# Moving batch 1's attention stretches within block 0, and summing four pairs' squares on ScalarE

## The chip, the core and the metric

The kernel runs on one core of a Trainium2 chip. The metric is the device time of one execution in microseconds (us): the median of three runs. One execution was also profiled, and all rows below come from that one.

Engines are named as in the profile: PE is TensorE (PEld its weight loads), DVE is VectorE, ACT is ScalarE, POOL is GpSimd, and SP is the engine whose queue issues most DMAs. Each engine takes its instructions strictly in the order in which they stand in its queue.

## The reference, cut to what matters

```python
# batch 8, heads 8, seq 576, head_dim 64, d_model 512, d_ff 2048, rank 32
kv  = einsum('bhsd,bhse->bhde', k, v)
out = einsum('bhsd,bhde->bhse', q, kv)
rms = sqrt(mean(out * out, axis=-1) + 1e-06)
x   = (out / rms * g_norm)            # then heads joined: (batch, 576, 512)
h   = x^T @ U @ V                     # mixes over the sequence, rank 32
u   = x + h^T
y   = u + maximum(u @ w_ch1, 0) @ w_ch2
```

The weights arrive as 64-bit floats and are decoded to 32-bit floats on the chip, then split in a high and a low part, so that each product takes three matmuls (high by high, high by low, low by high).

## The kernel before, in words

The 8 batches of 576 rows make 4608 rows, cut into blocks of 512. Blocks 0 to 2 are multiplied directly; the six later blocks in three stages by a scheme with seven products (names P1 to P7), whose weights are made during blocks 0 to 2 and stored to DRAM.

In blocks 0 to 2 a loop runs over the 16 chunks `f` of d_ff. One turn of it is 12 matmuls of the first layer of chunk `f` (lines L484 to L486 before), then relu and its remainder (`hh` on ACT at L496, `hl` on DVE at L501), then 12 matmuls of the second layer of chunk `f - 1` (L508). In block 0 the raw weights of a chunk are decoded during the loop, two to three chunks ahead: copies on ACT (`L167`, `L168`, and the high part `ws` at `L258`), and on DVE the steps L153 to L164 and the low part at `L262`. For chunks 10 and up SP also stores the decoded weights to DRAM (`wf`, L270); the buffer `dec` has two places in turn, so the copy that starts the decoding of chunk 12 waits for the store of chunk 10, and so on. Chunks 0 to 4 are worked off ahead of the loop in an order written out by hand. PE's order is the order of the code; the order on ACT and DVE is set by a list scheduler that works with its own estimate of the times.

Between these matmuls lies the attention of the next batches, pair of heads by pair. Pair (1, 2) is batch 1, heads 4 and 5. A *stretch* (`run(before, now, after)`) puts three things on PE one after another: the rank-32 product `t` of the pair before (L387, L390; it needs that pair's normalised `x`), the kv product of the pair after (L300) and the out product of the pair now (L319). Behind them ACT copies kv and out from PSUM (`kvb` L181, `x` L329), squares `x` into `xt` (L333), DVE sums the squares (L348), ACT takes the root and the half (L349, L350), DVE the reciprocal and one Newton step (L351, L343 to L345) and scales `x` (L363). DVE then turns `x` into the same `xt` (L377), and SP sends it through DRAM into `ut` (L380, L382). `t4_step` makes the factor `t` of the mix from the rank-32 product (ACT L400, L403, L405; DVE L401, L404, L406).

A *mix* (`mix_step`) is two matmuls of a pair's `t` with V (L463), whose results DVE adds to `ut` (L470), and a split of the sum (ACT L422, DVE L423). Stretches and mixes take turns with the two PSUM banks of one pool, so each waits until the one before has been read out.

A slot (j, n) of the tables RUNS and MIXES is the place in block j after quarter n of its chunks: n = 4f + i, where i = 0 is the middle of the first layer of chunk f, 1 its end, 2 the middle of the second-layer matmuls and 3 the end of the turn. From j = 3 on, n counts the units of the stages, of six matmuls each. The first entry of RUNS has no out product. So `t` of (1, 1) stands in the stretch named (1, 2), `t` of (1, 2) in the one named (1, 3), and `t` of (1, 3) in the one named (2, 0).

Of the kernel before, what the change touches and what calls it, by code (L numbers as in the profile page):

```python
# [10 lines left out]
F32 = mybir.dt.float32  # L11
# [4 lines left out]
AF = mybir.ActivationFunctionType  # L16
ALU = mybir.AluOpType
AX = mybir.AxisListType

B, H, S, D = 8, 8, 576, 64  # L20
DM, DF, R = 512, 2048, 32
P = 128
NPAIR = H // 2
NT = 5
# [8 lines left out]
QO = [0, 160, 320, 448]  # L33
ORDER = np.concatenate([np.arange(32) + P * i + 32 * a for a in range(4) for i in range(QL[a] // 32)])
NATIVE = 2
NC = 3
PAIRS = 3
KEEP = 4
FROM_DRAM = 5
COMBOS = [(1, f) for f in (1, 2, 4, 5, 7, 8, 10, 11, 13, 14)] + [(2, f) for f in (4, 5, 7, 8, 10, 11)]  # L40
RUNS = [((1, 0), (0, 20)), ((1, 1), (0, 28)), ((1, 2), (0, 37)), ((1, 3), (0, 45)), ((2, 0), (0, 54)),
# [4 lines left out]
MIXES = {(1, 0): ((0, 26),), (1, 1): ((0, 43),), (1, 2): ((0, 51),), (1, 3): ((0, 60),),  # L46
# [46 lines left out]
def build(ctx: ExitStack, tc: tile.TileContext, kv_in, kvt0_in, kvt_in, q_in, uv_in, g_in, w_in, out):  # L93
    nc = tc.nc
# [7 lines left out]
    sm = ctx.enter_context(tc.tile_pool(name="sm", bufs=2))  # L102
# [96 lines left out]
    def load_kv(b, p):  # L199
# [6 lines left out]
        nc.sync.dma_start(out=kt, in_=kv_in[b, p])  # L206
        if b >= NATIVE:
            tt = ldp.tile([P, 2 * P], F32, name="kvt_sb")
            nc.sync.dma_start(out=tt, in_=kvt_in[b - NATIVE, p])
            loads["t", b, p] = tt  # L210
# [91 lines left out]
    def kv_product(b, p, to):  # L302

        m = loads.pop(("kv", b, p))
        t = loads.pop(("t", b, p))
        by_heads(to, m, t, TAIL * (p % 2) if b < NATIVE else None)

    state = {}
# [16 lines left out]
    def squares(b, p):  # L325
        s = state[b, p]
        x = s["x"]
        for t, lo in zip(s["heads"], (0, D)):
            nc.scalar.activation(out=x[:, :, lo:lo + D], in_=t, func=AF.Copy if s["raw"] else AF.Square)  # L329
        if s["raw"]:  # L330
            xt = s["xt"] = sc.tile([P, 4, NT, 32], F32, name="xt")
            s["x2"] = xt.rearrange("p k i j -> p (k i j)").rearrange("p (i c) -> p i c", c=P)
            nc.scalar.activation(out=s["x2"], in_=x, func=AF.Square)  # L333

    def stats_parts(b, p):

        NS = 2 * NT
        sums, half, r0, ta = [sm.tile([P, NS], F32, name=n) for n in ("sums", "half", "r0", "ta")]
        xv = state[b, p]["x2"].rearrange("p i (h e) -> p i h e", e=D)
        state[b, p]["r"] = half.rearrange("p (i h) -> p i h", h=2)  # L340

        def newton():
            nc.vector.tensor_tensor(out=ta, in0=r0, in1=half, op=ALU.mult)  # L343
            nc.vector.tensor_tensor(out=ta, in0=ta, in1=r0, op=ALU.mult)
            nc.vector.scalar_tensor_tensor(out=half, in0=ta, scalar=1.5, in1=r0, op0=ALU.add, op1=ALU.mult)  # L345

        return dict(
            red=lambda: nc.vector.tensor_reduce(out=sums.rearrange("p (i h) -> p i h", h=2), in_=xv, axis=AX.X, op=ALU.add),  # L348
            ta=lambda: nc.scalar.activation(out=ta, in_=sums, func=AF.Sqrt, scale=1.0 / D, bias=eps[:, 0:1]),  # L349
            hf=lambda: nc.scalar.activation(out=half, in_=sums, func=AF.Identity, scale=-0.5 / D, bias=eps[:, 1:2]),  # L350
            rc=lambda: nc.vector.reciprocal(out=r0, in_=ta),  # L351
            nw=newton)
# [105 lines left out]
    def mix_part(b, p, part):  # L458
# [7 lines left out]
        if b > 2 and not (b in UPPER and part == 1):  # L466
            q = (S * b - BLK * NC) // (2 * BLK)
            at = S * b - BLK * NC - 2 * BLK * q
            to = x32(q)[p][:, at + lo:at + hi]
# [41 lines left out]
    def finish(y, j):  # L511
        uh, ul = ut[j]
        last_block = j == NC - 1
        kept = {}
# [27 lines left out]
    def x32(q):  # L542

        return [t[:, i] for t in x32_tiles(q) for i in range(2)]

    def carry(b, p):

        n = UPPER[b]
        q = (S * b + S - n - BLK * NC) // (2 * BLK)
        if b == 2:  # L550
# [161 lines left out]
    def end_unit(q, n, w):  # L712
# [17 lines left out]
        def leave(c, cols, queue):  # L730
            queue.dma_start(out=out[NC + 2 * q, 2 + c][:, cols], in_=ys[1][:, c, cols])

        if name != "P4":
            for c in range(2):
                products(c, slice(0, BLK), [(kk, w, hs)])
            if kk == KEEP - 1:
# [5 lines left out]
                if name == "P7":  # L742
                    nc.vector.tensor_tensor(out=ys[0], in0=ys[0], in1=spare("P5"), op=ALU.add)
                    for c in range(2):
                        nc.sync.dma_start(out=out[NC + 2 * q + 1, 2 + c], in_=ys[0][:, c])
            return
# [155 lines left out]
    def spread_v(n, eng):  # L902
# [4 lines left out]
        out=uv, in_=uvraw.bitcast(U32).rearrange("p (n t) -> p n t", t=2)[:, :, 1].bitcast(F32), func=AF.Abs)  # L907
# [153 lines left out]
    def run(before, now, after):  # L1061
# [4 lines left out]
        if after:  # L1066
            kv = (two if after[0] < NATIVE and after[1] % 2 else one)[:, BLK - D:]
            kv_product(*after, kv)
# [71 lines left out]
    for j in range(NC):  # L1140
# [3 lines left out]
        for f in range(FIRST if j == 0 else 0, NF):  # L1144
# [5 lines left out]
            h = (ps_h if f % 2 else pools["two"]).tile([P, BLK], F32, name="h")  # L1150
# [111 lines left out]
```

## Time and profile before

| | |
|---|---|
| median of three runs | 837.13 us (836.72 to 837.36) |
| the profiled execution's own time | 837.33 us |
| its span, first to last instruction | 835.6 us |
| PE busy | 820.7 us, 98% of the span, 5492 instructions |
| DVE busy | 585.4 us, 70% |
| ACT busy | 443.4 us, 53% |
| POOL busy | 80.3 us, 10% |
| mean granted TensorE clock | 0.995 |

The times of the runs are a little longer than the span, since they hold what lies ahead of the first instruction and behind the last. Shares of busy time are means over the whole span; the stages differ, so the rows below are cut out of block 0, where all but one of the moved pieces lie.

### The profile page before, as it was taken

The page shows a single profiled execution, that of the slowest core. Times are in us where ns is not written, and L with a number is a line of the kernel's source. Part 1 is how long each engine was busy: PE and PEld are TensorE (multiplying, and loading weights), DVE is VectorE, ACT ScalarE, POOL GpSimd, SP SyncE. Part 2 cuts the span into 40 slices and gives each one's busy share as a digit, 9 for nine tenths or more (in the row PEclk, how much of TensorE's full clock was granted, in tenths as well). Part 3 has the DMA queues.
Part 4 walks back from the last instruction along what each step waited for, and adds up shares of the span by engine and source line. Part 5 has one row for each costly group of instructions (what it writes and reads, how often), then busy time and mean ns, then how long its engine had stood idle before and what let it go on. Part 6 is the DMA issues. An engine that isn't in the chain of part 4 may idle for free.

```text
span 835.6 us, 14368 instructions
## 1 busy us (share of the span) xinstructions
PE 820.7 (98%) x5492; PEld 673.2 (81%) x5492; DVE 585.4 (70%) x1016; ACT 443.4 (53%) x810; POOL 80.3 (10%) x159
## 2 busy tenths in 40 slices
PE   8999799999999999999999999999999999999998
PEld 7777678888888888888888888788888888888887
DVE  5999885888776678666785688568736943582376
ACT  5978752544443445365645664656346724542462
POOL 3002214244330221000000000000000000000000
PEclk9999999999999999999999999999999999999999
DMA  9984767699887779467777768667555685555554
GB/s 346 415 340 144 225 200 226 219 321 277 262 252 266 239 214 316 160 236 262 241 264 236 264 238 282 231 204 242 178 187 196 207 281 197 182 196 195 202 200 153
DMA packets 66357, 198.39 MB, mean 237 GB/s; under 512 B 8176, under 2 KB 27376, under 8 KB 55536
## 3 DMA queue, kind: packets, MB, share of 16 engines
q1 hardware_dynamic: 57184, 167.97, 58.9%
q0 software_dynamic: 8960, 29.37, 10.5%
q8 instruction: 43, 0.70, 0.3%
q14 instruction: 26, 0.21, 0.1%
q10 hardware_dynamic: 144, 0.13, 0.0%
HBM read 146.84 MB, written 50.59 MB: 236 GB/s over the span
## 4 chain that ended last, share of the span: by engine, by line
PE 83%; DVE 6%; DMA 6%; ACT 3%; issue 1%; SPq 0%; ACTq 0%; DVEq 0%
PE yy L671 25%; PE yy L773 23%; PE y L508 13%; PE h L484 5%; PE h L485 5%; PE h L486 4%; DMA w1raw<-w_in 2%; PE ya L723 2%; DMA out<-x 1%; DMA raw<-w_in 1%; PE pp L300 1%; PE pp L319 1%; DVE dec L164 1%; PE h L300 1%; DVE uc L575 1%
## 5 line engine op out<-in xcount | busy, mean ns | idle before, releaser
L671 PE MATMUL yy<-uc,wt 128*128 128x512 f32 x1008 | 234.1, 391 | 0.9 <-ACT t L405 0.9
L671 PEld LDWEIGHTS yy<-uc,wt 128*128 128x128 f32 x1008 | 188.0, 188 | 40.7 <-ACT t L405 1.3
L773 PE MATMUL yy<-dec,wt 128*128 128x512 f32 x468 | 113.8, 391 | 0.3 <-DVE dec L662 0.3
L508 PE MATMUL y<-hh,ws 128*128 128x512 f32 x336 | 113.4, 393 | 0.0
L773 PE MATMUL yy<-hh,wt 128*128 128x512 f32 x312 | 103.3, 390 | 0.0
L773 PEld LDWEIGHTS yy<-dec,wt 128*128 128x128 f32 x468 | 87.2, 188 | 18.9 <-DVE dec L662 0.7
L662 DVE TENSOR_TENSOR hl<-hk,hh 128x512 fp32r<-128x512 f32 x72 | 48.1, 686 | 39.7 <-ACT hh L701 39.5
L662 DVE TENSOR_TENSOR dec<-hk,dec 128x512 fp32r<-128x512 f32 x72 | 48.9, 686 | 37.1 <-ACT dec L701 36.7
L508 PEld LDWEIGHTS y<-hh,ws 128*128 128x128 f32 x336 | 63.1, 188 | 13.8
L773 PEld LDWEIGHTS yy<-hh,wt 128*128 128x128 f32 x312 | 58.6, 188 | 12.4
L484 PE MATMUL h<-ut,ws 128*128 128x512 f32 x168 | 67.5, 402 | 0.0
L485 PE MATMUL h<-ut,ws 128*128 128x512 f32 x168 | 66.6, 396 | 0.0
L486 PE MATMUL h<-ut,ws 128*128 128x512 f32 x168 | 66.4, 395 | 0.0
L508 PE MATMUL y<-hl,ws 128*128 128x512 f32 x168 | 65.8, 391 | 0.0
L773 PE MATMUL yy<-hl,wt 128*128 128x512 f32 x156 | 60.7, 389 | 0.0
L701 ACT CAST dec<-hk 128x512 fp32r<-128x512 f32 x72 | 44.2, 621 | 29.0 <-PE yy L773 14.9
L701 ACT CAST hh<-hk 128x512 fp32r<-128x512 f32 x72 | 44.0, 622 | 27.0 <-PE yy L773 22.8
L659 ACT COPY sp<-yy 128x1024 f32<-128x1024 f32 x35 | 35.5, 1014 | 32.6 <-PE yy L671 25.3
L496 ACT ACTIVATE hh<-h 128x512 fp32r<-128x512 f32 x48 | 28.4, 591 | 36.8 <-PE h L486 36.6
L684 ACT ACTIVATE hk<-hk 128x1024 f32<-128x1024 f32 x24 | 25.5, 1061 | 36.3 <-DVE hk L683 36.3
L659 ACT COPY yy<-yy 128x1024 f32<-128x1024 f32 x17 | 17.0, 998 | 43.4 <-PE yy L671 40.5
L501 DVE SCALAR_TENSOR_TENSOR hl<-h,hh 128x512 fp32r<-128x512 f32 x48 | 32.7, 682 | 9.4 <-ACT hh L496 9.4
(237 smaller groups left out, 1348.0 us busy)
## 6 DMA issues: line engine op xcount, KB each, us to landing
wt<-wd SPq DMA_DIRECT2D x84, 1024.0 KB, 4.9
kv_sb<-kv_in SPq DMA_DIRECT2D x29, 512.0 KB, 5.9
raw<-w_in SPq DMA_DIRECT2D x14, 1023.6 KB, 14.9
wd<-dec POOLq DMA_DIRECT2D x44, 256.0 KB, 5.7
wd<-ws POOLq DMA_DIRECT2D x42, 256.0 KB, 4.0
q_sb<-q_in SPq DMA_DIRECT2D x29, 288.0 KB, 6.3
ut<-xd SPq DMA_DIRECT2D x28, 288.0 KB, 4.1
out<-x SPq DMA_DIRECT2D x23, 256.0 KB, 4.6
```

The source lines that it names most:

```text
L484: nc.tensor.matmul(h, lhsT=w1s[f][0][:, d, :], rhs=uh[d], start=(n == 0), stop=False)
L485: nc.tensor.matmul(h, lhsT=w1s[f][0][:, d, :], rhs=ul[d], start=False, stop=False)
L486: nc.tensor.matmul(h, lhsT=w1s[f][1][:, d, :], rhs=uh[d], start=False, stop=(n == ND - 1))
L496: last["relu"] = nc.scalar.activation(out=last["hh"], in_=h, func=AF.Relu)
L501: last["low"] = nc.vector.scalar_tensor_tensor(out=hl, in0=h, scalar=0.0, in1=last["hh"].bitcast(F32), op0=ALU.max, op1=ALU.subtract)
L508: nc.tensor.matmul(acc, lhsT=w2s[f][w][:, c, :], rhs=h[:, cols], start=(f == 0 and w == 0 and h is hh), stop=(f == NF - 1 and w == 1))
L659: last["unit"] = nc.scalar.copy(out=pair_bank("P6") if name == "P1" else spare(name), in_=acc)
L662: return nc.vector.tensor_tensor(out=out, in0=a, in1=b, op=ALU.subtract)
L671: nc.tensor.matmul(acc[:, i], lhsT=w[:, ws_, e * P:(e + 1) * P], rhs=u[:, e, us], start=name in ("P1", "P5") and e == 0 and k == 0, stop=e ...
L684: last["unit"] = nc.scalar.activation(out=to, in_=to if other else acc, func=AF.Relu)
L701: last["unit"] = nc.scalar.copy(out=hh, in_=src)
L773: nc.tensor.matmul(acc[:, c], lhsT=w[:, ws_, c * P:(c + 1) * P], rhs=h, start=name in ("P1", "P5") and kk == 0 and i == 0, stop=kk == KEEP ...
```

## The change

Three tables and two functions change. In RUNS four stretches of block 0 move to earlier slots: (1, 1) from 28 to 25, (1, 2) from 37 to 33, (1, 3) from 45 to 41 and (2, 0) from 54 to 50; in stage 4 the stretch (7, 2) moves from 18 to 20. In MIXES the mixes of batch 1 move to later slots: 26 to 30, 43 to 45, 51 to 54 and 60 to 61. For the four pairs in SUMMED the one square over 128 x 640 and the sum on DVE are replaced by ten squares over 128 x 64 on ACT, each of which also gives the sum of its 64 results.

```diff
+SUMMED = ((1, 1), (1, 2), (1, 3), (2, 0))
...
-RUNS = [((1, 0), (0, 20)), ((1, 1), (0, 28)), ((1, 2), (0, 37)), ((1, 3), (0, 45)), ((2, 0), (0, 54)),
+RUNS = [((1, 0), (0, 20)), ((1, 1), (0, 25)), ((1, 2), (0, 33)), ((1, 3), (0, 41)), ((2, 0), (0, 50)),
...
-        ((6, 3), (3, 72)), ((7, 0), (3, 84)), ((7, 1), (4, 7)), ((7, 2), (4, 18)), ((7, 3), (4, 29)), (None, (4, 40))]
-MIXES = {(1, 0): ((0, 26),), (1, 1): ((0, 43),), (1, 2): ((0, 51),), (1, 3): ((0, 60),),
+        ((6, 3), (3, 72)), ((7, 0), (3, 84)), ((7, 1), (4, 7)), ((7, 2), (4, 20)), ((7, 3), (4, 29)), (None, (4, 40))]
+MIXES = {(1, 0): ((0, 30),), (1, 1): ((0, 45),), (1, 2): ((0, 54),), (1, 3): ((0, 61),),
...
-            nc.scalar.activation(out=s["x2"], in_=x, func=AF.Square)
+            if (b, p) not in SUMMED:
+                nc.scalar.activation(out=s["x2"], in_=x, func=AF.Square)
+                return
+            sums = s["sums"] = sm.tile([P, 2 * NT], F32, name="sums")
+            for i in range(NT):
+                for h in range(2):
+                    part = slice(h * D, (h + 1) * D)
+                    nc.scalar.activation(out=s["x2"][:, i, part], in_=x[:, i, part], func=AF.Square,
+                                         accum_out=sums[:, 2 * i + h:2 * i + h + 1])
...
-            red=lambda: nc.vector.tensor_reduce(out=sums.rearrange("p (i h) -> p i h", h=2), in_=xv, axis=AX.X, op=ALU.add),
+            red=lambda: summed or nc.vector.tensor_reduce(out=sums.rearrange("p (i h) -> p i h", h=2), in_=xv, axis=AX.X, op=ALU.add),
```

The new code shifts the lines behind it: the relu is L496 before and L507 in the change, the scaling of `x` L363 and L374, the low part `ws` L262 and L263.

On ACT, this is what stands behind the kvb copies of the stretch named (1, 1) before (`raw_412` is the raw weights of chunk 10, `raw_414` of chunk 11; `ws_939` is chunk 9):

```order
L181 COPY kvb_99<-pp 64x64 x2
L329 ACTIVATE x_89<-pp 128x5x64 x2
L258 CAST ws_939<-dec 128x1024
L333 ACTIVATE xt<-x_89 128x640
L496 ACTIVATE hh<-h 128x512
L167 COPY dec<-raw_414 128x1024
L168 COPY top<-dec 128x1024
L349 ACTIVATE ta<-sums,eps 128x10
L350 ACTIVATE half<-sums,eps 128x10
```

and in the change (chunk 9 is `ws_999` here):

```order
L182 COPY kvb_99<-pp 64x64 x2
L330 ACTIVATE x_89<-pp 128x5x64 x2
L168 COPY dec<-raw_412 128x1024
L341 ACTIVATE xt,sums<-x_89 128x64 x10
L259 CAST ws_999<-dec 128x1024
L169 COPY top<-dec 128x1024
L360 ACTIVATE ta<-sums,eps 128x10
L361 ACTIVATE half<-sums,eps 128x10
L507 ACTIVATE hh<-h 128x512
```

The copy that starts chunk 10 now stands ahead of the squares, and the ten squares ahead of the cast of chunk 9.

On DVE, the scaling of pair (1, 1)'s `x` (L363 before) is reached through these rows before (`r_991` is the pair's reciprocal):

```order
L343 TENSOR_TENSOR ta<-r_991,half 128x10
L160 SCALAR_TENSOR_TENSOR dec<-dec 128x256
L344 TENSOR_TENSOR ta<-ta,r_991 128x10
L262 TENSOR_TENSOR ws_1046<-dec,ws_1046 128x1024
L345 SCALAR_TENSOR_TENSOR half<-ta,r_991 128x10
L164 SCALAR_TENSOR_TENSOR dec<-raw_414,top 128x1024
L363 TENSOR_TENSOR x_89<-x_89,half 128x640
```

and in the change, where the scaling is L374 and the reciprocal `r_960` (ahead of the first of these rows stand, from the low part of chunk 9 on, that part, the join of chunk 10, the reciprocal and `hl` of chunk 7):

```order
L481 TENSOR_TENSOR ut_90<-pp,ut_90 128x288 x2
L354 TENSOR_TENSOR ta<-r_960,half 128x10
L154 TENSOR_SCALAR dec<-dec 128x256
L263 TENSOR_TENSOR ws_1054<-dec,ws_1054 128x1024
L355 TENSOR_TENSOR ta<-ta,r_960 128x10
L155 TENSOR_SCALAR dec<-dec 128x1024
L434 SCALAR_TENSOR_TENSOR ut<-ut_90,g_sb,ut 128x448
L356 SCALAR_TENSOR_TENSOR half<-ta,r_960 128x10
L159 TENSOR_SCALAR dec<-dec 128x256
L154 TENSOR_SCALAR dec<-dec 128x256
L374 TENSOR_TENSOR x_89<-x_89,half 128x640
```

The sums and the split of the mix of (1, 0) (L481, L434) and two further decode steps now lie between the reciprocal and the scaling; the second L154 is the first DVE step of chunk 12.

For pair (1, 2), these rows of DVE end in its scaling in the change; `hl` at L512 is that of chunk 10, the chunk whose first layer is the last thing on PE ahead of `t` of (1, 2) in slot 41:

```order
L355 TENSOR_TENSOR ta<-ta,r_1143 128x10
L159 TENSOR_SCALAR dec<-dec 128x256
L512 SCALAR_TENSOR_TENSOR hl<-h,hh 128x512
L356 SCALAR_TENSOR_TENSOR half<-ta,r_1143 128x10
L161 SCALAR_TENSOR_TENSOR dec<-dec 128x256
L374 TENSOR_TENSOR x_88<-x_88,half 128x640
```

So the scaling of (1, 2) has moved to a place behind the remainder of chunk 10; before, its last `hl` ahead of it was that of the same chunk 10 too, but `t` of (1, 2) stood a whole turn of 24 matmuls later on PE.

## Rows read from the trace of the kernel before

**Rows 1.** Windows: busy us and count of PE, PEld, DVE, ACT, POOL; PEclk; DMA.

```profile
102.00:104.00 2.00, 2.00 (x6) 1.71 (x7) 1.85 (x7) 2.00 (x3) 1.95 (x3) 0.50 0.73 259
70.00:120.00 50.00, 43.25 (x357) 34.33 (x357) 42.77 (x79) 37.10 (x59) 8.76 (x14) 0.93 0.64 205
120.00:340.00 220.00, 220.00 (x1791) 179.88 (x1790) 164.52 (x357) 95.75 (x232) 63.85 (x112) 1.00 0.80 255
```

**Rows 2.** What PE waited for, from 60 to 130 us: total, times, longest.

```profile
PE pp L463 <- DVE t L406: 4.8, 2, 3.4
PE pp L387 <- DVE x L363: 1.2, 1, 1.2
PE pp L300 <- DVE ut L470: 0.8, 1, 0.8
```

**Rows 3.** Timeline of PE: start, us, instruction, idle before and its releaser.

```profile
81.20 0.39 PE L508 MATMUL y<-hh,ws 128*128 128x512 f32 x1
81.43 0.39 PE L508 MATMUL y<-hl,ws 128*128 128x512 f32 x1
...
101.78 0.82 PE L463 MATMUL pp<-v,t 128*128 128x288 f32 x2 [3.42 <-DVE t L406]
102.39 0.63 PE L484 MATMUL h<-ut,ws 128*128 128x512 f32 x1
...
107.60 0.43 PE L387 MATMUL pp<-x,uf 128*32 128x128 f32 x8
...
123.94 0.42 PE L387 MATMUL pp<-x,uf 128*32 128x128 f32 x8
```

**Rows 4.** Timeline of ACT.

```profile
72.22 1.05 ACT L258 CAST ws<-dec 128x1024 fp32r<-128x1024 f32 x1 [1.56 <-DVE dec L164]
...
73.74 1.35 ACT L168 COPY top<-dec 128x1024 uint8<-128x1024 uint8 x1
...
76.41 0.77 ACT L329 ACTIVATE x<-pp 128x320 f32<-128x320 f32 x2
...
78.00 0.74 ACT L333 ACTIVATE xt<-x 128x640 f32<-128x640 f32 x1
...
86.31 1.13 ACT L167 COPY dec<-raw 128x1024 uint8<-128x1024 uint8 x1 [0.48 <-DMA wf<-dec]
```

**Rows 5.** Timeline of DVE.

```profile
79.62 0.81 DVE L348 TENSOR_REDUCE sums<-xt 128x10 f32<-128x640 f32 x1
...
81.88 1.22 DVE L164 SCALAR_TENSOR_TENSOR dec<-raw,top 128x1024 uint32<-128x1024 uint32 x1
...
87.00 0.82 DVE L363 TENSOR_TENSOR x<-x,half 128x640 f32<-128x640 f32 x1
```

**Rows 6.** Groups by form, ACT from 20, DVE from 60, to 250 us: busy, mean ns.

```profile
L496 ACT ACTIVATE hh<-h 128x512 fp32r<-128x512 f32 x33 | 19.5, 591 | 23.0 <-PE h L486 22.9
L181 ACT COPY kvb<-pp 64x64 f32<-64x64 f32 x26 | 5.4, 206 | 8.3 <-PE pp L319 8.0
L1044 ACT CAST ut<-ut 128x64 fp32r<-128x64 f32 x4 | 1.0, 241 | 0.0
...
L501 DVE SCALAR_TENSOR_TENSOR hl<-h,hh 128x512 fp32r<-128x512 f32 x28 | 19.1, 682 | 4.5 <-ACT hh L496 4.5
L262 DVE TENSOR_TENSOR ws<-dec,ws 128x1024 fp32r<-128x1024 f32 x10 | 12.2, 1223 | 2.8 <-ACT ws L258 2.7
L154 DVE TENSOR_SCALAR dec<-dec 128x1024 uint8<-128x1024 uint8 x8 | 5.7, 717 | 0.2
L470 DVE TENSOR_TENSOR ut<-pp,ut 128x288 f32<-128x288 f32 x8 | 3.2, 444 | 1.2 <-PE pp L463 1.2
L423 DVE SCALAR_TENSOR_TENSOR ut<-ut,g_sb,ut 128x448 fp32r<-128x448 f32 x4 | 2.7, 679 | 1.5 <-ACT ut L422 1.5
```

**Rows 7.** Timelines of DVE and PE in stage 4, around pair (7, 1).

```profile
571.35 0.28 DVE L406 TENSOR_TENSOR t<-two,t 64x128 fp32r<-64x128 f32 x1
573.19 0.29 PE L463 MATMUL big<-v,t 128*128 128x288 f32 x1
```

More of the change, by code (lines that the diff above doesn't have):

```diff
@@ L332, in squares @@
             s["x2"] = xt.rearrange("p k i j -> p (k i j)").rearrange("p (i c) -> p i c", c=P)
-            nc.scalar.activation(out=s["x2"], in_=x, func=AF.Square)
+            if (b, p) not in SUMMED:
[7 more added lines that the diff above has]
+                                         accum_out=sums[:, 2 * i + h:2 * i + h + 1])
     def stats_parts(b, p):
         NS = 2 * NT
-        sums, half, r0, ta = [sm.tile([P, NS], F32, name=n) for n in ("sums", "half", "r0", "ta")]
+        half, r0, ta = [sm.tile([P, NS], F32, name=n) for n in ("half", "r0", "ta")]
+        summed = "sums" in state[b, p]
+        sums = state[b, p]["sums"] if summed else sm.tile([P, NS], F32, name="sums")
         xv = state[b, p]["x2"].rearrange("p i (h e) -> p i h e", e=D)
```

## The prediction, made before the change was timed

> **What bounds the kernel now.** I read the windows first. PE is busy without a gap from 120 to 340 us, but for only 43.25 of the 50 us from 70 to 120, at a mean clock of 0.93 [rows 1]. So something can be won in block 0 alone. The waits of PE name the places: two mixes that wait for their factor `t`, 4.8 us together; one rank-32 product that waits for the scaled `x`, 1.2; one stretch that waits for a bank that a mix's sum still reads, 0.8 [rows 2]. In the timeline of PE the longest, 3.42 us, ends at 101.78, and the clock is 0.50 behind it, the lower of its two levels, 1.2 GHz [rows 1, 3]: the 12 matmuls and the gap between 102.39 and 107.60 take 5.2 us, where 12 take 2.7 at the usual step of 0.227 (81.20 to 81.43 shows it rounded) [rows 3]. That costs another 2.5. Waits and clock together are 9.3 us, 1.1% of the time, and the most that the change can win. In the same window DVE is busy for 42.8 and ACT for 37.1 of 50 us [rows 1]: both have little room, and whatever stands ahead of a pair's scaling in their queues delays it.
>
> **The change, part by part.** A matmul step on PE does not change; what counts is when `x` of a pair is scaled, since the pair's rank-32 product holds up all of PE behind it.
>
> *When ACT can square (1, 1).* Up to the cast of chunk 8, ACT's queue is unchanged, so that cast ends at 73.27 as before [rows 4]. Behind it now stand a copy to `top` (1.35), two kvb copies of 0.206, the two copies of `x` (0.77) and the copy that starts a chunk (1.13) [rows 4, 6]: 3.66, less about 0.3 for the overlap of neighbours. The ten squares start near 76.6, not at 78.00 [rows 4], though the stretch is 4 us earlier on PE.
>
> *What ten squares cost.* No row has an ACTIVATE that also gives a sum. The nearest is the 128x64 cast, 0.241 us: ten are 2.4 [rows 6]. Not less than the one pass over the same 640 columns, 0.74 [rows 4]; if delivering each sum costs as much again as a small copy (0.206), ten are 4.5 [rows 4, 6]. I take 2.4, since the shape is that of the cast and neighbours overlap a little. They end near 79.0.
>
> The Trainium skill ("ScalarE: Activation LUTs", "What ACT_TABLE_LOAD costs") gives an ACTIVATE 186 ns plus 0.833 ns a column and lets neighbours overlap by 93 ns; worked out as an estimate, that is 0.15 us for each of a row and 1.5 for ten, and every later time of the pair would move forward by 0.9. The same section says nothing on the price of the sum, and the trace before cannot either.
>
> *When DVE can scale (1, 1).* The sum's 0.81 [rows 5] is gone, but the queue ahead of the scaling has grown. From the end of the squares: cast of chunk 9, 1.05; its low part, 1.22; join of chunk 10, 1.22; reciprocal, about 0.2; `hl`, 0.68; the two sums of mix (1, 0), 0.81 to 0.89; low part of chunk 10, 1.22; a clamp, 0.72; the split of the mix, 0.68; six small steps of Newton and decoding, some 0.2 each (an estimate), 1.3; the scaling, 0.82 [rows 4 to 6]. That makes 9.9; with 0.9 off for 14 overlaps of neighbours, 9.0. `x` is ready at 88.0, against 87.82 before [rows 5]. The store of chunk 10 gives the same: the join ends at 82.5; before, the copy two chunks on began 3.2 us behind the end of the join (83.10 to 86.31) [rows 4, 5], so now at 85.8; its 1.13, DVE's first step of that chunk and the scaling end at 88.1. Both ways meet.
>
> PE reaches this product early: it has then done what it had done at 81.20 [rows 3], less the 0.8 wait for the bank, so it stands at 80.4 and waits **7.7 us**. Before, it had 24 matmuls more behind it by this product, 5.4 us. Lateness: 5.4 + 0.2 = **+5.6**.
>
> *Clock.* A wait of 3.42 was followed by the lower level [rows 1, 3]; I take the same **+2.5** behind the longer one.
>
> *`t` of (1, 2).* The waits at the two mixes and the clock behind the first are gone: the mixes are now 12 and 13 quarters behind their stretch instead of 6: **-3.4, -2.5** and, below, -1.4. But in slot 41 the product follows directly on the first layer of chunk 10, while DVE scales (1, 2) only behind that chunk's `hl`. So PE must wait for relu 0.59, `hl` 0.68, two small steps 0.5 and scaling 0.82 [rows 5, 6], with hand-overs **+2.9**, whatever ACT and DVE did before. Lateness: 5.6 + 2.5 + 2.9 - 3.4 - 2.5 = 5.1; the product starts at 107.60 + 5.1 less 24 matmuls and a mix, 5.8, so at 106.9.
>
> *`t` of (1, 3).* From 107.60 to 123.94 PE needed 16.3 us before, with 1.4 of waiting (the second of the 4.8) [rows 2, 3]; the work between the two products is the same now. ACT and DVE need more: join of chunk 13 to 108.1; the store's 3.2 and the copy of chunk 15 to 112.4; cast of 14 to 113.4; then ten squares 2.4, `top` 1.35, cast of 15 1.05 and some 3 us of the stretch's small copies (0.2 to 0.4 each) to 120.8; on DVE a low part 1.22, small steps 0.9, two sums 0.85, `hl` 0.68, scaling 0.82, less overlaps, to 124.6 [rows 4 to 6]. That is 17.7, so PE waits 2.8 instead of 1.4, part of it where mix (1, 1) wants the bank of the stretch: **+1.4**.
>
> *Stage 4.* `t` of (7, 1) was ready at 571.63, 1.56 ahead of its mix at 573.19 [rows 7]. It now starts two units, 12 matmuls or 2.7 us, later, and the mix stays: **+1.2**.
>
> *At no cost.* The loads of the moved stretches are issued as soon as the stretch before frees its buffer, so they move along; PE waited for none from 60 to 130 [rows 2], and were one late, it would eat into the 7.7 first. The mix of (1, 3) has 11 quarters and waits for nothing. Sums no longer on DVE, 4 x 0.81, are counted in the times above.
>
> Sum: 5.6 + 2.5 + 2.9 - 3.4 - 2.5 + 1.4 + 1.2 = +7.7 on 837.33, the profiled execution's own time, which is 0.2 above the median: **845.0 us**. Behind block 0 PE has no idle time in which to make it up [rows 1].
>
> **The rivals.** *Faster.* All four waits and the clock's loss go and nothing comes in their place: 837.3 - 9.3 = 828.0. For it: every stretch is earlier, the mixes later, and the fuller engine, DVE, loses 3.3 us of sums. It decides if (1, 1) is scaled by 80.4; up to 83.0 the change still pays, since a lateness of 0.6 and then 2.5 + 2.9 + 1.2 are as much as the 3.4 + 2.5 + 1.4 that go. Against it: even free squares leave 85.6 by the queue above. The Trainium skill ("Perfetto Trace Analysis", "Optimizing Scalar/DVE Operations") holds that work may well be offloaded to Scalar where DVE is saturated; by that rule the time would be this rival's 828.0. Of the trace, the shares agree with it, the queue does not. Chance 0.12.
>
> *No change.* Squares as cheap as one pass (0.74) put (1, 1) at 86.3: lateness 3.9; the clock stays up: no 2.5; the wait at (1, 2) is 2.7 and the one at (1, 3) nothing: 3.9 + 2.7 - 3.4 - 2.5 - 1.4 + 1.2 = +0.5, 837.8. For it: shorter waits than 3.42 left the clock alone. Against: 7 us is longer. Chance 0.07.
>
> *Dear squares.* At 4.5 for ten, each of three pairs comes 2.1 later, in a row on the same queues: +6.3, 851.3. For it: a sum that must be fetched is an instruction of its own. Chance 0.19.
>
> **How the numbers follow.** The forecast, 845.0, has 0.62 and its own range of 841 to 849 (1 us on each of four terms). Leaving out the fast rival and part of the ends, the range is 838.5 to 852. Within 0.2% (1.7 us, about what can be told from no change here) lies only the rival without change: faster 0.12, same 0.07, slower 0.81.
>
> **What would show it.** PE waits some 7 to 8 us for the scaling near 80, with the clock at 0.5 behind it; 3 us near 103 for the scaling of (1, 2); no waits for `t` in block 0's mixes; ten squares of 2.4 us. It is wrong if the scaling of (1, 1) ends before 83, if the sums cost far from 0.24 each, or if the stages behind block 0 change by more than 1 to 2 us.

## The result and the profile after

The changed kernel takes 846.41 us (median of 4 runs, 844.53 to 847.44) against 837.25 for the kernel before: ratio 1.0108, 95% interval 1.0093 to 1.0122, so it is slower, by some 9 us. Its profiled execution took 845.74 us, with a span of 843.9 (835.6 before). Lines of the kernel after stand up to 11 higher than those of before.

The windows of the profile after (columns as in [rows 1]) put the loss into block 0: PE is busy for 38.1 of the 50 us from 70 to 120, where it was 43.3, and the granted clock is at its lower level in two stretches instead of one.

```profile
70.00:120.00 50.00, 38.09 (x275) 30.84 (x274) 37.17 (x67) 38.62 (x109) 8.89 (x14) 0.86 0.59 192
120.00:340.00 220.00, 219.41 (x1787) 179.03 (x1786) 160.35 (x351) 97.33 (x253) 64.08 (x112) 1.00 0.78 248
88.00:90.00 2.00, 2.00 (x35) 1.67 (x38) 2.00 (x4) 1.34 (x1) 0.00 (x0) 0.50 0.04 12
...
110.00:112.00 2.00, 2.00 (x6) 1.53 (x5) 0.74 (x1) 0.00 (x0) 0.00 (x0) 0.50 0.92 247
```

What PE waited for from 60 to 135 us answers to [rows 2]. The mixes' waits for `t` are gone; the products wait for the scaled `x` instead, 10.9 us in two waits.

```profile
PE pp L398 <- DVE x L374: 10.9, 2, 7.4
PE pp L474 <- ACT x L330: 1.0, 1, 1.0
PE y L519 <- DVE hl L512: 0.6, 1, 0.6
```

The timeline of PE shows the products of (1, 1), (1, 2) and (1, 3). Their starts are to be held against 87.97 (in the same timeline of before, the first row below), 107.60 and 123.94 [rows 3]: the same, 1.4 us sooner and 1.8 us later, though 24 matmuls fewer (5.4 us) stand ahead of each.

```profile
87.97 0.42 PE L387 MATMUL pp<-x,uf 128*32 128x128 f32 x8 [1.17 <-DVE x L363]
```

```profile
87.98 0.66 PE L398 MATMUL pp<-x,uf 128*32 128x128 f32 x8 [7.45 <-DVE x L374]
...
106.16 0.66 PE L398 MATMUL pp<-x,uf 128*32 128x128 f32 x8 [3.41 <-DVE x L374]
...
117.73 0.40 PE L474 MATMUL pp<-v,t 128*128 128x288 f32 x1 [1.05 <-ACT x L330]
...
125.77 0.43 PE L398 MATMUL pp<-x,uf 128*32 128x128 f32 x8
```

The timeline of ACT has the ten squares, each followed by an instruction of its own that reads the sum. For (1, 1) they stand together and end at 78.85, where the cast starts. For (1, 3) five of them stand between the two copies of `x` out of PSUM (L330): the second copy, on which a bank hangs, starts 2.4 us behind the first, where [rows 4] show both as one row of 0.77.

```profile
76.44 0.28 ACT L341 ACTIVATE xt<-x 128x64 f32<-128x64 f32 x1
76.60 0.21 ACT L341 ACTIVATION_READ_ACCUMULATOR xt<-x 128x1 f32 x1
76.70 0.27 ACT L341 ACTIVATE xt<-x 128x64 f32<-128x64 f32 x1
...
78.85 1.05 ACT L259 CAST ws<-dec 128x1024 fp32r<-128x1024 f32 x1
...
114.82 0.44 ACT L330 ACTIVATE x<-pp 128x320 f32<-128x320 f32 x1
115.29 0.26 ACT L341 ACTIVATE xt<-x 128x64 f32<-128x64 f32 x1
...
117.24 0.44 ACT L330 ACTIVATE x<-pp 128x320 f32<-128x320 f32 x1
```

### The profile page after: what moved, and what is told of

Its sections match the earlier page's. It is cut to its first block, busy times and chain, and to the rows that moved or that the text cites. A ratio compares the mean times of both kernels' runs of the same rounds, so it can differ in the third digit from the quotient of the medians.

```text
span 843.9 us, 14438 instructions
## 1 busy us (share of the span) xinstructions
PE 823.2 (98%) x5492; PEld 675.2 (80%) x5492; DVE 582.4 (69%) x1012; ACT 450.6 (53%) x886; POOL 80.7 (10%) x159
## 4 chain that ended last, share of the span: by engine, by line
PE 80%; DVE 8%; DMA 5%; ACT 5%; issue 1%; SPq 0%; ACTq 0%; DVEq 0%
PE yy L682 24%; PE yy L784 22%; PE y L519 13%; PE h L495 4%; PE h L496 4%; PE h L497 4%; DMA w1raw<-w_in 2%; PE ya L734 2%; DMA out<-x 1%; DMA raw<-w_in 1%; PE pp L301 1%; PE pp L320 1%; DVE ws L263 1%; ACT xt L341 1%; DVE dec L165 1%
## 5 line engine op out<-in xcount | busy, mean ns | idle before, releaser
L495 PE MATMUL h<-ut,ws 128*128 128x512 f32 x168 | 66.4, 395 | 0.1
L496 PE MATMUL h<-ut,ws 128*128 128x512 f32 x168 | 65.6, 390 | 0.0
L497 PE MATMUL h<-ut,ws 128*128 128x512 f32 x168 | 65.4, 389 | 0.0
L507 ACT ACTIVATE hh<-h 128x512 fp32r<-128x512 f32 x48 | 28.5, 594 | 40.9 <-PE h L497 40.6
L512 DVE SCALAR_TENSOR_TENSOR hl<-h,hh 128x512 fp32r<-128x512 f32 x48 | 32.7, 681 | 9.9 <-ACT hh L507 9.8
```

Source lines behind the costliest of these rows:

```text
L495: nc.tensor.matmul(h, lhsT=w1s[f][0][:, d, :], rhs=uh[d], start=(n == 0), stop=False)
L496: nc.tensor.matmul(h, lhsT=w1s[f][0][:, d, :], rhs=ul[d], start=False, stop=False)
L497: nc.tensor.matmul(h, lhsT=w1s[f][1][:, d, :], rhs=uh[d], start=False, stop=(n == ND - 1))
L507: last["relu"] = nc.scalar.activation(out=last["hh"], in_=h, func=AF.Relu)
L512: last["low"] = nc.vector.scalar_tensor_tensor(out=hl, in0=h, scalar=0.0, in1=last["hh"].bitcast(F32), op0=ALU.max, op1=ALU.subtract)
```

## The experiments

All ran beside the kernel before, whose medians in the three sets were 836.48, 836.80 and 836.53 us. Times are medians; "product" is PE's rank-32 product of a pair. The starts, and all rows, are those of one profiled execution, which took up to 1.7 us less (after_scaled_first) and up to 3.3 us more (only_sums) than its run's median.

| run | time, ratio to before (95%) | products of (1, 1), (1, 2), (1, 3) start at |
|---|---|---|
| only_sums | 840.82, 1.0060 (1.0038 to 1.0082) | 87.38, 107.95, 129.34 |
| only_tables | 841.51, 1.0057 (1.0040 to 1.0074) | 83.92, 105.70, 122.10 |
| first_plain | 846.60, 1.0111 (1.0092 to 1.0130) | 84.72, 105.45, 122.69 |
| first_summed | 840.16, 1.0039 (1.0025 to 1.0052) | 89.60, 105.68, 121.16 |
| mixes_only | 842.55, 1.0072 (1.0056 to 1.0088) | 87.31, 106.00, 127.17 |
| mixes_mid | 833.86, 0.9963 (0.9950 to 0.9977) | 88.68, 104.43, 120.64 |
| mid_scaled_first | 831.97, 0.9940 (0.9919 to 0.9961) | 89.23, 102.29, 119.43 |
| mid_tuned | 833.12, 0.9956 (0.9940 to 0.9971) | 89.02, 102.80, 121.58 |
| mid_summed | 836.98, 1.0001 (0.9991 to 1.0011) | 89.54, 103.18, 123.05 |
| after_scaled_first | 840.18, 1.0044 (1.0028 to 1.0060) | 83.03, 99.68, 118.08 |
| warm_waits | 849.10, 1.0147 (1.0125 to 1.0169) | 95.82, 114.93, 130.00 |
| warm_short | 848.22, 1.0129 (1.0109 to 1.0149) | 88.12, 106.12, 126.10 |

The first theory, in the expectations of the first set, was that the ten squares are dear because of the place that the scheduler then gives the scaling.

**only_tables**, the changed kernel without the sums:

```diff
-SUMMED = ((1, 1), (1, 2), (1, 3), (2, 0))
+SUMMED = ()
```

> The changed kernel with its tables, but no pair in SUMMED: one pass of squares (0.74 us) and the sum on DVE (0.81) again. Ledger for all runs: 828.0 us is the kernel before without its waits and clock loss of block 0 (837.3 - 9.3); the changed kernel is that plus its waits and clock losses, 7.45 + 1.8 + 3.41 + 2.7 + 1.6 + 0.8 = 17.8, or 845.8. Theory (order): the ten squares are dear because the scheduler, which sees them end later, sets the scaling of (1, 1) on DVE behind the join of chunk 10, hl, the sums of mix (1, 0) and the low part of chunk 10; without them its order puts the scaling ahead of these, only a low part (1.23) and small steps behind the sum. Then x of (1, 1) is scaled at about 81.9 instead of 87.9, PE waits about 1.4 instead of 7.45, the clock stays up, and the waits behind it are 0 to 2 and 0 to 1.6: 830 to 834 us, faster than before. Rival (tables): a stretch at slot 25 is too early whatever the squares are: wait of 5.5 to 7.5 there, 842 to 846. Rival (price): only the ScalarE time of the ten squares counts, 1.7 a pair: wait of 5.7, clock lost as now, some 842.

The place moved as the theory said: `x` of (1, 1) is scaled at 80.94 instead of 87.11 (timeline of DVE of this run, first three rows). But the product still waits 3.50, for a bank with the sums of mix (1, 0) (L481), and what is won is lost at (1, 2) with a wait of 7.17 (timeline of PE, last two):

```profile
80.94 0.82 DVE L374 TENSOR_TENSOR x<-x,half 128x640 f32<-128x640 f32 x1
...
83.42 0.45 DVE L481 TENSOR_TENSOR ut<-pp,ut 128x288 f32<-128x288 f32 x1
...
104.74 0.82 DVE L374 TENSOR_TENSOR x<-x,half 128x640 f32<-128x640 f32 x1
```

```profile
83.92 0.43 PE L398 MATMUL pp<-x,uf 128*32 128x128 f32 x8 [3.50 <-DVE ut L481]
...
105.70 0.66 PE L398 MATMUL pp<-x,uf 128*32 128x128 f32 x8 [7.17 <-DVE x L374]
```

The time misses the theory's 830 to 834 and falls just short of the rival's 842 to 846. The two waits make 10.7 us, those of the changed kernel at the same products 10.9.

**first_plain** and **first_summed** part the four pairs (first_summed ran in the last set, when the theory of a fixed time, told further down, was there):

```diff
-SUMMED = ((1, 1), (1, 2), (1, 3), (2, 0))
+SUMMED = ((1, 2), (1, 3), (2, 0))   # first_plain
+SUMMED = ((1, 1),)                  # first_summed
```

> The changed kernel with (1, 1) alone taken out of SUMMED; the other three pairs keep their ten squares. Theory (order): the wait for x of (1, 1) falls from 7.45 to about 1.4 and the clock stays up there; the scaling of (1, 2) still stands behind hl of chunk 10 on DVE, so that wait stays at 2.5 to 3.4, with or without a clock loss of 2.7: 834 to 837.5. Rival (tables): 842 to 846. Rival (price): 1.7 less than the changed kernel, 844.

> The changed kernel with the ten squares for (1, 1) alone; the other three pairs have one pass of squares and the sum on DVE. It completes the table: no pair summed 841.5, all but (1, 1) 846.6, all four 846.4. Theory (fixed time, and the ten squares of the later pairs split the two copies of x from PSUM): the wait at (1, 1) is 7.45 as in the changed kernel and the one at (1, 2) 3 to 3.5, since the scaling of (1, 2) comes at 104 to 106 in any case; but no square stands between the two copies of (1, 3) and (2, 0), so no mix waits for a bank: 841 to 843.5. Rival (additive): the sums of (1, 1) alone cost the 3.9 us by which 7.45 is longer than the 3.50 without, 845 to 846.5.

Without the sums of (1, 1) the time stays, 846.60 against 846.41, though the wait there is 3.48 instead of 7.45. With them alone the wait is 7.42 and the time 840.16, no worse than with none (841.51). first_summed and only_tables differ in these sums alone: at the product of (1, 1) first_summed is 5.7 us later, at that of (1, 2) level (105.68 and 105.70). So the longest wait of the kernel costs nothing by itself; the sums of the later three pairs cost 5 to 6 us. The additive rival falls. The other comparison shows less: first_plain is still 3.1 us ahead of the changed kernel at the product of (1, 3), and loses that only behind it. There five squares of (2, 0) stand between the two copies and wait 4.39 us for the DMAs that read the only buffer `xt`; behind them the second copy, its bank and mix (1, 2) are late, which makes PE wait 3.12.

**only_sums**, the kernel before with the sums:

> The kernel before with its own tables, and the ten squares with accumulators for the four pairs. Theory (order): a later place for the squares costs here too, but less, since the stretch of (1, 1) is 3 slots later: the squares are done near 81.3 instead of 78.7, x of (1, 1) is scaled near 88.5 to 89 instead of 87.82, the wait for it is 1.9 to 2.5 instead of 1.2; t for the mixes comes about 0 to 1.5 later: 838 to 841 us. Rival (price): four pairs at 1.7 each on the path, 842 to 844. Rival (tables): no change, 836.5 to 838, since sums on ScalarE take 0.81 a pair off the fuller engine.

The median is at the theory's end of the range: 4.3 us, about what the sums cost on the new tables (846.41 - 841.51 = 4.9). Waits of mixes for `t` are 6.9 us in its profiled execution, which took 844.14, and 4.8 before [rows 2].

**mixes_only**, the kernel before with the later mixes:

```diff
-MIXES = {(1, 0): ((0, 26),), (1, 1): ((0, 43),), (1, 2): ((0, 51),), (1, 3): ((0, 60),),
+MIXES = {(1, 0): ((0, 30),), (1, 1): ((0, 45),), (1, 2): ((0, 54),), (1, 3): ((0, 61),),
```

> The kernel before (its stretches, no ten squares, stage 4 as it was) with the later mixes of block 0 alone. Theory: the mixes' waits for t (4.8), the clock behind the longer (2.5) and the wait for the bank (0.8) go, the wait for x of (1, 1) stays at about 1.2, and nothing new comes, since the scalings keep their places: 829 to 832 us, faster than both kernels. Rival: later mixes fill DVE and ACT when the next pairs are scaled, and the waits turn up at the stretches (2 to 4 us there): 832 to 836. Rival (tables and squares play no part, later mixes cost): over 837.

A miss: 6.1 us slower, beyond the first rival's range too; of the three only "over 837" holds it. The mixes' waits go, and PE waits 5.59 for `x` of (1, 2) at 106.00, and 3.6 more at mixes for a bank, all but 0.34 of it at the two that now stand in the slot of a stretch. Yet `x` of (1, 2) is not later than before: it is scaled at 105.04 (106.27 there), and the product starts 1.6 us sooner than in the kernel before; PE was only there earlier. The loss lies behind this product. From it to that of (1, 3) the run takes 21.2 us where before takes 16.3, with nearly the same waits in between (1.8 and 1.4 us), but with the clock at its lower level for most of the way (window of mixes_only; before is at 1.00 from 108 on). Worked out from these, some 4.4 us are the clock's.

```profile
106.00:118.00 12.00, 10.18 (x89) 8.16 (x90) 11.29 (x20) 9.55 (x18) 0.00 (x0) 0.51 0.58 175
```

Why `x` is no earlier, though PE waits for it, is seen in the timelines of this run, DVE first, then ACT: the small steps of Newton are done to the last but one at 101.95, then a join (L165) stands ahead of the last (L356), and then the first step of chunk 14's decode (L154) ahead of the scaling. That step waits for the copy L168 on ACT, which waits for the store of chunk 12. The store is issued at 95.17 behind the loads of the next pair and lands 8.5 us later, the longest of four (last fence: all stores of this run from 75 to 112).

```profile
101.78 0.17 DVE L355 TENSOR_TENSOR ta<-ta,r 128x10 f32<-128x10 f32 x1
102.14 1.23 DVE L165 SCALAR_TENSOR_TENSOR dec<-raw,top 128x1024 uint32<-128x1024 uint32 x1 [0.19 <-ACT top L169]
103.28 0.16 DVE L356 SCALAR_TENSOR_TENSOR half<-ta,r 128x10 f32<-128x10 f32 x1
104.83 0.29 DVE L154 TENSOR_SCALAR dec<-dec 128x256 uint32<-128x256 uint32 x1 [1.38 <-ACT dec L168]
105.04 0.81 DVE L374 TENSOR_TENSOR x<-x,half 128x640 f32<-128x640 f32 x1
```

```profile
103.70 1.09 ACT L168 COPY dec<-raw 128x1024 uint8<-128x1024 uint8 x1 [1.60 <-DMA wf<-dec]
```

```profile
DMA to landing us min/median/max: 3.4/4.5/8.5
```

The additive theory has now fallen in several runs. What they share is (1, 2): its scaling starts between 104.5 and 107.1 in before, after and these five. The second theory: that time is fixed, since in the queues it stands behind decode steps that wait for a store; it is not fixed by PE.

The traces bear out the place behind decode steps, but the store only in some runs. A copy ahead of the scaling waits for a store until 103.70 in mixes_only, 104.08 in only_sums and 99.32 in only_tables. In the changed kernel ACT waits for none from 86 to 109. There DVE works without a gap from 99.51 to the scaling of (1, 2) at 105.20, and 3.5 us of it are decode steps of two chunks. The `hl` of chunk 10 is in this row, but does not set the time either: its relu is done at 103.38, and DVE comes to it only at 104.18 (timelines of after, DVE, then ACT).

```profile
99.51 1.23 DVE L263 TENSOR_TENSOR ws<-dec,ws 128x1024 fp32r<-128x1024 f32 x1 [0.74 <-ACT ws L259]
...
102.17 0.21 DVE L362 RECIPROCAL r<-ta 128x10 f32<-128x10 f32 x1
...
104.18 0.68 DVE L512 SCALAR_TENSOR_TENSOR hl<-h,hh 128x512 fp32r<-128x512 f32 x1
104.78 0.15 DVE L356 SCALAR_TENSOR_TENSOR half<-ta,r 128x10 f32<-128x10 f32 x1
104.86 0.41 DVE L161 SCALAR_TENSOR_TENSOR dec<-dec 128x256 uint32<-128x256 uint32 x1
105.20 0.81 DVE L374 TENSOR_TENSOR x<-x,half 128x640 f32<-128x640 f32 x1
```

```profile
102.78 0.60 ACT L507 ACTIVATE hh<-h 128x512 fp32r<-128x512 f32 x1 [0.47 <-PE h L497]
```

So what holds `x` of (1, 2) is the decode that the queues have ahead of it, whether it waits for a store or is work.

**mixes_mid** and **mid_scaled_first** test it on the kernel before. The first puts each mix between two stretches. The second also queues the decode of chunk 13 behind the square root and the scaling of (1, 2), of chunk 15 behind those of (1, 3); `scaled` keeps those two instructions:

```diff
-MIXES = {(1, 0): ((0, 26),), (1, 1): ((0, 43),), (1, 2): ((0, 51),), (1, 3): ((0, 60),),
+MIXES = {(1, 0): ((0, 24),), (1, 1): ((0, 50),), (1, 2): ((0, 58),), (1, 3): ((0, 62),),
+BEHIND = {13: (1, 2), 15: (1, 3)}    # mid_scaled_first alone, here and below
...
+                    with ExitStack() as behind:
+                        for ins in scaled.get(BEHIND.get(ahead), []):
+                            behind.enter_context(tc.issue_after(ins))
                         for what in decode_w(ahead).values():
                             what()
```

> The kernel before with its stretches, no ten squares, and the four mixes of block 0 in the middle between two stretches (slots 24, 50, 58, 62). In the run with the later mixes alone the four waits of mixes for a bank were 3.6 us and one for the sums 0.6; they came from mixes that stand in the slot of a stretch, and go here. The wait for the scaled x of (1, 2), 5.6 there, stays. New theory (fixed time): in the kernel before, the changed one and four variants the scaling of (1, 2) starts between 104.5 and 107.1 us, however early PE is, because it stands on DVE and ACT behind decode steps that wait for the store of a chunk two back; what is won ahead of it is waited off there. So: x of (1, 2) again at 104 to 106, PE waits 4 to 5.5 for it with the clock at 0.5 behind, 837 to 840 us, no faster than before. Rival (additive): each wait is worth its length, so without the mixes' waits 830 to 833.

> The same, and the decode of chunk 13 is queued on ACT and DVE behind the square root and the scaling of (1, 2), that of chunk 15 behind those of (1, 3). No work is added or taken away. New theory (fixed time set by the order): nothing that waits for a store stands ahead of the scaling any more; x of (1, 2) is scaled at 99 to 102 instead of 104 to 106, the wait there is 0 to 2 and the clock stays up, and the chunks are needed some 10 us later than they come: 829 to 834 us, faster than before. Rival (decode is the bound): chunks 13 to 15 come later by what the pair gains, PE waits for their weights instead, and the time is that of the run without the new order, 837 to 841.

mixes_mid is faster than forecast, 0.4% below before: the product of (1, 2) waits 2.63, not 4 to 5.5, since `x` is scaled at 103.46 and PE is there later; the fixed time had moved by a microsecond or more. mid_scaled_first came as the theory said: no decode step stands between Newton's steps and the scaling, which starts at 100.94 (timeline of DVE), the product does not wait, and the copy that does wait for a store, 3.38 us, stands behind it (timeline of ACT). The clock is 1.00 throughout.

```profile
100.05 0.17 DVE L356 TENSOR_TENSOR ta<-ta,r 128x10 f32<-128x10 f32 x1
100.14 0.68 DVE L518 SCALAR_TENSOR_TENSOR hl<-h,hh 128x512 fp32r<-128x512 f32 x1
100.74 0.16 DVE L357 SCALAR_TENSOR_TENSOR half<-ta,r 128x10 f32<-128x10 f32 x1
100.94 0.82 DVE L379 TENSOR_TENSOR x<-x,half 128x640 f32<-128x640 f32 x1
```

```profile
103.33 1.14 ACT L169 COPY dec<-raw 128x1024 uint8<-128x1024 uint8 x1 [3.38 <-DMA wf<-dec]
```

It is the fastest kernel of all, 0.994 of before. The two intervals against before overlap (from 0.9950 to 0.9961), but both kernels ran in the same set, and run against run the order takes 1.9 us more off than the mixes alone (95% interval 0.7 to 3.2, from 6 and 11 runs); the profile shows the wait of 2.63 gone.

**after_scaled_first** puts the same order into the changed kernel, with `BEHIND = {10: (1, 1), 12: (1, 2), 14: (1, 3)}`:

> The changed kernel as it is, ten squares and tables included, with the decode of chunk 10 queued on ACT and DVE behind the square root and scaling of (1, 1), that of chunk 12 behind those of (1, 2), of chunk 14 behind those of (1, 3). New theory: x of (1, 1) is scaled near 82.8 instead of 87.9; the product then waits for the bank of mix (1, 0), whose sums are freed near 84.5, so 4 us instead of 7.45; the scaling of (1, 2) comes 11 us behind the end of its stretch, near 98, wait 0 to 2 instead of 3.4, no clock loss there: 833 to 838 us. Rival (ten squares are too dear in any order): 842 or more. Rival (decode is the bound): PE waits for weights of chunks 12 to 14, 842 or more.

The scalings come at 80.78, 98.71 and 117.21 instead of 87.11, 105.20 and 124.46; the waits are 2.71 (the bank), 2.03 and 2.74, and once 0.57 for the weights of a chunk. The time is 6.2 us lower than the changed kernel's, but 2 above the theory's range: early stretches still wait.

**mid_summed** and **mid_tuned** change the fastest kernel, by the sums and by two mixes a slot later (25 and 51):

> The fastest kernel so far (before's stretches, mixes at 24, 50, 58, 62, chunks 13 and 15 behind the scalings; 832.0) with the ten squares for the four pairs: what they are worth where no stretch is early and nothing waits for a store ahead of the scaling. Theory: they take 3.3 us off DVE but wait for nothing less; the first five of (1, 3) and (2, 0) stand between the two copies of x, so the second copy and the bank come 1.2 us or more later and the mixes wait for it: 833 to 836. Rival (DVE is the fuller engine, so any work off it gains): 829 to 831.

> The fastest kernel so far (832.0) with two mixes one slot later, 25 and 51: its waits left in block 0 are 2.2 us of mix (1, 0) for t and 1.4 of mix (1, 1) for a bank. A slot is 6 matmuls of 0.227 us, 1.4. Theory: 0.8 of the first is left, none of the second, nothing new: 829 to 831. Rival: the sums of mix (1, 0) now hold the bank that the stretch at slot 28 needs, and what is won is waited off there: 831.5 to 833.

The sums cost 5.0 us on the fastest kernel. The timeline of ACT of mid_summed shows them between the copies of (1, 3), with a cast and a copy of decode behind them; the timeline of PE shows mix (1, 1) wait for the second copy, 3.34 where it was 1.38:

```profile
110.57 0.44 ACT L331 ACTIVATE x<-pp 128x320 f32<-128x320 f32 x1
111.04 0.26 ACT L342 ACTIVATE xt<-x 128x64 f32<-128x64 f32 x1
...
112.26 1.03 ACT L260 CAST ws<-dec 128x1024 fp32r<-128x1024 f32 x1
113.19 1.33 ACT L170 COPY top<-dec 128x1024 uint8<-128x1024 uint8 x1
...
115.17 0.44 ACT L331 ACTIVATE x<-pp 128x320 f32<-128x320 f32 x1
```

```profile
115.66 0.42 PE L480 MATMUL pp<-v,t 128*128 128x288 f32 x1 [3.34 <-ACT x L331]
```

Behind that wait the clock is at its lower level (0.50 from 116 to 118), and by the product of (1, 3) 3.6 of the 5.0 us are lost (123.05 against 119.43). DVE is busy for 37.6 us from 70 to 120 instead of 42.7, 2.5 of the difference being sums that are gone and the rest work that now falls behind 120; nothing comes of it.

mid_tuned cannot be told from mid_scaled_first (the intervals overlap), and 833.12 is above the theory's range and just above the rival's. The wait for `t` falls to 0.8 as the theory said, but the mixes' waits for a bank grow from 1.4 to 2.0, and 0.7, 0.7 and 1.3 appear at two products and a second layer. So what is won is waited off, as the rival had it, but not at the place that it named.

**warm_waits** and **warm_short** fill PE's two waits in the changed kernel with matmuls of zeros:

```diff
+        for _ in range(WARM.get(now, 0)):     # {(1, 2): 44, (1, 3): 20}; short: 12 and 10
+            nc.tensor.matmul(two[:, NT * D:NT * D + P], lhsT=zeros, rhs=zeros, start=True, stop=True)
         if before:
```

> The changed kernel with matmuls of zeros on PE while it waits, 44 ahead of the product of (1, 1) and 20 ahead of that of (1, 2), at about 0.13 us each 5.7 and 2.6 us, less than the waits of 7.45 and 3.41. They change no result. It measures the clock's share. If they keep the clock up: the 1.8 behind the first wait and the 2.7 behind the second are not lost. Theory (fixed time of the scaling of (1, 2)): the first 1.8 goes into a longer wait at (1, 2), the second is kept: 843 (842 to 844). Rival (additive): 841.5. Rival (the clock falls for another reason than the wait): 845 to 847.

> As the run with matmuls of zeros, but 12 and 10 of them: there each took 0.266 us (88 rows, 11.72 us) and not 0.13, and they started behind the release of a bank at 84.2, so that 44 kept PE busy until 95.9 where x was ready at 88. Twelve end at 87.4 and ten, from 102.8, at 105.4, ahead of the scaled x both times. Theory (the clock follows the wait, the time of the scaling of (1, 2) is fixed): the 1.8 behind the first wait goes into the second, the 2.7 behind the second is kept, 842.5 to 844.5. Rival (additive): 841 to 842.5. Rival (the clock has another cause): 845 to 847.5.

The first run tells little: each call gave two rows of 0.133 us, and PE was late by its own filling. In the second the clock is up when both products start and behind them (windows of warm_short):

```profile
84.00:88.00 4.00, 4.00 (x23) 3.98 (x22) 4.00 (x10) 2.23 (x4) 0.96 (x2) 0.57 0.92 307
88.00:92.00 4.00, 4.00 (x83) 3.32 (x82) 3.96 (x8) 1.88 (x2) 0.00 (x0) 1.00 0.40 129
...
108.00:112.00 4.00, 4.00 (x26) 3.30 (x18) 2.91 (x4) 2.42 (x6) 0.53 (x1) 1.00 1.00 247
```

Yet the products of (1, 2) and (1, 3) start at 106.12 and 126.10, where the changed kernel has them at 106.16 and 125.77, because `x` is scaled at 105.16 (105.20 there) and 125.23. PE was ready for the product of (1, 2) 1.5 us sooner (its last matmul ahead, zeros aside, starts at 100.82 instead of 102.36). So up to here not even the second clock loss was on the path, against the theory too. The run's median is 1.8 us above the changed kernel's, with intervals that overlap; its profiled execution is 3.5 above, and its trace shows where: PE waits 2.81 us for `x` of (1, 3), and the clock is at its lower level behind that product (window of warm_short), where it is 1.00 in the changed kernel. The stretch and the six matmuls behind it take 6.0 us instead of 3.4.

```profile
126.00:132.00 6.00, 5.90 (x78) 4.96 (x79) 1.46 (x4) 2.33 (x10) 0.79 (x2) 0.50 0.86 249
```

## Why the prediction was right

The time came within 1.4 us of the forecast, and so did the lateness at each place: at the products of (1, 1), (1, 2) and (1, 3) and at the end 5.6, 5.1, 6.5 and 7.7 us were forecast, and 5.5, 4.5, 7.7 and 8.3 came. But the sum's terms do not add as it had them. It counts each wait and each clock loss as a price of its own, while most of what PE loses at one product is given back at the next, where `x` comes at a time that PE does not set. That the total is so near is in part luck.

- **Squares.** Start 76.6, measured 76.44; ten in 2.4, measured 76.44 to 78.85. Right, by another way than thought: 249 ns for the square and 193 for reading the sum, overlapping to a step of 0.24 (last section). The Trainium skill ("ScalarE: Activation LUTs", "What ACT_TABLE_LOAD costs") led to an estimate of 0.15 a square, without a price for reading the sum; the rows say 0.24 for both, and they decide.
- **Scaling of (1, 1).** 88.0 forecast, 87.11 measured; wait 7.7, measured 7.45. Right in size. Wrong in worth: the +5.6 of lateness is no loss of its own, as first_summed beside only_tables shows. "Even free squares leave 85.6" was wrong as well: in only_tables the scheduler orders DVE anew, and the scaling starts at 80.94. Nor does the change pay if (1, 1) is scaled by 83.0: there it is, at 81.76, and the time is 5.0 us above before.
- **Clock.** +2.5 behind the first wait; the stretch took 3.9 us (87.98 to 91.89) where warm_short took 2.3 with the clock up, 1.7 less. A second loss, behind 106.16, was not foreseen. In effect the term is nothing here: in warm_short, without both losses, the product of (1, 3) starts no sooner. Where no later `x` makes PE wait anyway, a clock loss does count, as warm_short shows behind 126 and mixes_only behind 106.
- **(1, 2).** Wait 2.9 and start 106.9, measured 3.41 and 106.16. The size is right, the reason fell: DVE comes to the `hl` of chunk 10 only 0.8 us after its relu is done. In warm_short PE came 1.5 sooner and `x` was no earlier, though there that chunk's relu starts only at 105.08, so that its `hl` is not even ahead of the scaling. With the decode behind the scaling (after_scaled_first), `x` is scaled 6.5 us sooner. The step that failed is "whatever ACT and DVE did before".
- **Mixes.** Their waits for `t` are gone, as forecast; but -3.4 and -2.5 are not won by that alone: mixes_only, with the same mix slots on the stretches of before, has neither wait and is 6.1 us slower. No run has the changed kernel with the mixes at their old slots.
- **(1, 3).** A wait of 2.8 forecast; 1.05 for the bank and 0.59 for `hl`, 1.64.
- **Stage 4.** +1.2 forecast, 0.82 measured, and from the wrong rows: [rows 7] are those of the next pair. The moved stretch's mix stood at 556.51 in before, its `t` ready at 554.62 (554.33 and 0.29); 2.7 later leaves a wait of 0.8.

In place of the sum the runs show this. The product of (1, 2) starts at 106.16 where it started at 107.60, with 24 matmuls (5.45 us at 0.227) and a mix (0.45) less done: 5.9 - 1.44 = +4.5. In only_tables it starts at 105.70, +4.0, so this part is the tables. From there to the product of (1, 3) the same work takes 19.6 us instead of 16.3: +3.3, where only_tables takes 16.4; this part is the sums, with which `x` of (1, 3) is scaled at 124.46 instead of 121.23. Stage 4 adds 0.8. Together 8.6, against 8.3 between the spans. So the tables and the sums share the loss, as only_tables (+5.0) and only_sums (+4.3) say by themselves.

Of the rivals, the fast one is what would follow from the rule of the Trainium skill ("Perfetto Trace Analysis", "Optimizing Scalar/DVE Operations") that work may be offloaded from a saturated DVE to Scalar. mid_summed speaks against it here, where DVE is busy for 42.7 of 50 us: four sums of 0.81 us leave DVE, and 5.0 us are lost. "Dear squares" had the wrong mechanism: each costs what the forecast took, and by the rows of mid_summed and first_plain it is the place between the two copies that costs. No run keeps the ten squares behind both copies, so this is read from the rows and not tested by itself.

What is left of the loss with the decode behind the scalings is not explained to the end: after_scaled_first wins 6.2 of 9.2 us, and still waits at all three products.

## What to carry to other kernels

A long wait is worth its length only if what follows is not held by something else: before pricing it, look up when the next product's operand was ready, and whether that moves when the engine comes earlier. Read the queue ahead of a late instruction for work that is not needed yet, whether it waits for a DMA or keeps the engine busy. Moving it behind gave 6.2 us on the changed kernel, and 1.9 on the kernel before on top of 2.9 from mixes halfway between the stretches; the tables without the sums (only_tables) gave a loss of 5.0. An instruction cut into ten can be spread by a scheduler, so ask what now stands in front of the copy that frees a bank.

## What the runs showed of the hardware

An ACTIVATE with a sum leaves a second instruction, which no instruction of the kernel's text shows (groups by form, ACT, 60 to 140 us of the profile after):

```profile
L341 ACT ACTIVATE xt<-x 128x64 f32<-128x64 f32 x40 | 9.7, 249 | 1.7 <-DMA xd<-xt 1.7
...
L341 ACT ACTIVATION_READ_ACCUMULATOR xt<-x 128x1 f32 x40 | 7.7, 193 | 0.0
```

The lower clock came with a delay. In only_tables PE resumes at 83.92 at the upper level, after a wait of 3.50, and the level falls behind that (windows of only_tables from 84 to 88):

```profile
84.00:86.00 2.00, 2.00 (x64) 1.84 (x68) 2.00 (x5) 1.58 (x3) 1.66 (x3) 0.74 0.61 215
86.00:88.00 2.00, 2.00 (x22) 1.59 (x17) 2.00 (x4) 0.14 (x1) 0.00 (x0) 0.50 1.04 319
```

In warm_short the zeros begin at 83.60 after 2.93 us without work and take the slow stretch on themselves (0.57 from 84 to 88); the product at 88.12 finds the clock at 1.00. So they did not keep the clock up at the first wait, as the expectation had it, but they let it recover before the work that counts.

A store of 512 KB took from 3.4 to 8.5 us in one run (mixes_only); why is not shown. A queue that holds such a wait ahead of the pair's steps passes this spread on to PE.
